# Fewer dummy products around the first transposes of a gated attention and SwiGLU kernel

## Chip, cores and metric

The kernel runs on one core of a Trainium2 chip. The metric is the device time of one execution in microseconds (us), lower is better. Before the change: 180.97 us, median of the three runs known when the prediction was written (180.55 to 181.46).

## The reference, cut to what matters

```python
def reference(A_x, A_wqkv, A_wo, B_x, B_w1, B_w3, B_w2, gate_w):
    x = A_x                                   # 1 x 2048 x 512, bf16
    g = sigmoid((x * gate_w).sum(-1, keepdims=True))
    a = linear_attention(x, A_wqkv, A_wo)     # q, k, v; phi(k)^T v and phi(q), 32 heads
    b = swiglu(x, B_w1, B_w3, B_w2)           # 512 -> 1376 -> 512
    return g * a + (1 - g) * b
```

Only the very first step counts here: keys of the first four token tiles, `k = x @ wk`, with x transposed on TensorE.

## The kernel before

Loads are issued on two queues. The first transposes need token tile 0 of x, the first key product needs the transposed tile and the first half of `wk`.

```python
dq = nc.sync
dq.dma_start(out=x_sb[:, 0:1, :], in_=x_r[:, 0:1, :])            # x tile 0
for i in range(2):                                               # wk, two halves
    kcs = slice(2 * i, 2 * i + 2)
    nc.scalar.dma_start(out=wk_sb[:, kcs, :], in_=wqkv_r[:, kcs, D : 2 * D])
dq.dma_start(out=x_sb[:, 1:2, :], in_=x_r[:, 1:2, :])            # x tile 1
dq.dma_start(out=x_sb[:, 2:TPB, :], in_=x_r[:, 2:TPB, :])        # x tiles 2 and 3
# ... later loads cut
warm_l = nc.const_aps.tensor(1.0, [P, P], BF16)
warm_r = nc.const_aps.tensor(1.0, [P, TB], BF16)                 # P = 128, TB = 512

def emit_warm(n):                                                # dummy products
    warm = psX.tile([P, TB], FP32, tag="XP3", name="warm")
    for i in range(n):
        nc.tensor.matmul(warm[:], lhsT=warm_l, rhs=warm_r, start=True, stop=True)

emit_warm(6)

def emit_xT(t):                  # 4 transposes of tile t, two copies back to SBUF
    for h in range(2):
        xTp = psX.tile([P, 2, P], BF16, tag=f"XP{(2 * t + h) % 3}", name="xTp")
        for j in range(2):
            kc = 2 * h + j
            nc.tensor.transpose(
                out=xTp[:, j, :], in_=x_sb[:, t, kc * P : (kc + 1) * P], identity=ident[:]
            )
        # ... h == 0: copy on VectorE, h == 1: copy on ScalarE
# ... cut
k0 = [psM.tile([P, D], FP32, tag="mm", name=f"k0_{t}") for t in range(TPB)]
emit_xT(0)
emit_warm(2)
emit_k_mm(k0[0], 0, 0)           # one product of 512 columns each
emit_k_mm(k0[0], 0, 1)
emit_xT(1)
emit_k_mm(k0[0], 0, 2)           # needs the second half of wk
emit_k_mm(k0[0], 0, 3)
emit_k_phi(k0[0], 0)
emit_xT(2)                       # needs x tiles 2 and 3, which land together
# ... then k tile 1, transposes of tile 3, k tiles 2 and 3, then the XP products (x^T @ phi(k))
```

TensorE (PE) starts its products in this order, so a step that waits holds up all those below it (in the trace before, the transposes of tile 0 wait until 3.41 us, and the two dummies below them, which need no load, start at 3.81).

## Time and profile before

Lines of the page of the kernel before. The second is the busy share of PE in 40 slices, in tenths; the third the granted clock; the last is the chain that ended last, by engine. PEld is TensorE's weight load, DVE is VectorE, ACT ScalarE, POOL GpSimd.

```profile
PE 175.5 (98%) x892; PEld 84.5 (47%) x892; DVE 118.9 (66%) x205; ACT 66.7 (37%) x126; POOL 61.2 (34%) x69
...
PE   8999999999999999999999999999999999999993
...
PEclk9999999999999999999999999999999999999999
...
PE 98%; DVE 0%; issue 0%; DVEq 0%
```

PE is the bound from end to end; only what moves its stream counts. One trap: the clock row says 9 in the first slice too, although the products there ran at half speed. The trace's clock record begins only at 5.88 us, and what lies before it is shown as if at full speed. The distance between starts tells the truth: 0.427 us for products before it, 0.216 after.

The timeline of the same kernel's start: start and duration in us, engine, line, operation, output and inputs, count, and in brackets the idle time before and what ended it.

```profile
0.84 2.72 PE L158 MATMUL warm<-const-bfloat16-1.0 128*128 128x512 bf16 x6 [0.84 <-PEq L471]
...
3.40 0.34 PEld L169 LDWEIGHTS <-x_sb 128*128 128x128 bf16 x4 [0.75 <-DMA x_sb<-in_A_x_dram]
3.41 0.61 PE L169 MATMUL xTp<-ident,x_sb 128*128 128x128 bf16 x4
...
3.81 1.06 PE L158 MATMUL warm<-const-bfloat16-1.0 128*128 128x512 bf16 x2
3.84 0.29 DVE L174 COPY xT<-xTp 128x256 bf16<-128x256 bf16 x1 [2.78 <-PE xTp L169]
...
4.66 1.06 PE L179 MATMUL k<-wk_sb,xT 128*128 128x512 bf16 x2
...
5.51 0.56 PE L169 MATMUL xTp<-ident,x_sb 128*128 128x128 bf16 x4
...
5.92 0.59 PE L179 MATMUL k<-wk_sb,xT 128*128 128x512 bf16 x2
...
6.35 0.39 PE L169 MATMUL xTp<-ident,x_sb 128*128 128x128 bf16 x4
```

Read the starts, since the durations include a modelled tail. Six dummies (0.84), four transposes (3.41), two dummies (3.81), the first two key products (4.66), transposes of tile 1 (5.51), two key products (5.92), transposes of tile 2 (6.35). Up to 5.8 us a product of 512 columns follows the last after 0.427 us and a transpose after 0.107; at full clock these are 0.216 and 0.056.

### The profile page before, as it was taken

What the parts mean: (1) busy time and instruction counts of PE and PEld (TensorE: products, weight loads), DVE (VectorE), ACT (ScalarE), POOL (GpSimd) and SP (SyncE); (2) the same over time, 40 slices, a digit from 0 to 9 for tenths busy, and PEclk for the clock granted to TensorE, in tenths of its full rate; (3) what the DMA queues carried; (4) which work ended last, traced back from release to release, by engine and by line L of the source; (5) the groups of instructions that cost most, each with busy time, mean ns of one, the idle gap of its engine ahead of it and who ended that gap; (6) DMA issues with size and microseconds to landing.
All of it is one profiled execution on the core that took longest, in us unless ns stands there. A gap on an engine that the chain in (4) does not pass through costs nothing.

```text
span 179.3 us, 2484 instructions
## 1 busy us (share of the span) xinstructions
PE 175.5 (98%) x892; PEld 84.5 (47%) x892; DVE 118.9 (66%) x205; ACT 66.7 (37%) x126; POOL 61.2 (34%) x69
## 2 busy tenths in 40 slices
PE   8999999999999999999999999999999999999993
PEld 3544444474444545444445444444545444444462
DVE  1598868596998837397787374978754669776000
ACT  4543322576624334343324343332443323331221
POOL 5177575645454323253003232620032328100000
PEclk9999999999999999999999999999999999999999
DMA  5999999901005010115000101240001013300011
GB/s 176 262 246 228 293 313 390 309 18 25 10 0 106 13 48 29 44 42 104 0 4 0 44 32 41 59 90 5 0 7 57 16 62 65 60 0 0 29 52 42
DMA packets 28285, 14.88 MB, mean 83 GB/s; under 512 B 19600, under 2 KB 27248, under 8 KB 28272
## 3 DMA queue, kind: packets, MB, share of 16 engines
q1 hardware_dynamic: 27728, 14.20, 29.5%
q10 hardware_dynamic: 544, 0.52, 0.8%
q8 instruction: 7, 0.11, 0.3%
q14 instruction: 6, 0.05, 0.1%
HBM read 8.42 MB, written 2.10 MB: 59 GB/s over the span
## 4 chain that ended last, share of the span: by engine, by line
PE 98%; DVE 0%; issue 0%; DVEq 0%
PE o_ps L350 19%; PE gate_ps L305 19%; PE up_ps L313 19%; PE XP L199 8%; PE o_ps L341 8%; PE q_ps L212 8%; PE k_ps L179 6%; PE r_ps L236 3%; PE k L179 2%; PE warm L158 2%; PE o_ps L345 2%; PE xTp L169 1%; PE kvT_ps L411 0%; PE W_ps L438 0%; DVE o_out L359 0%; PE z_ps L429 0%
## 5 line engine op out<-in xcount | busy, mean ns | idle before, releaser
L305 PE MATMUL gate_ps<-xT,w_sb 128*128 128x512 bf16 x160 | 41.1, 379 | 0.0
L313 PE MATMUL up_ps<-xT,w_sb 128*128 128x512 bf16 x160 | 41.1, 379 | 0.0
L220 POOL TENSOR_TENSOR qz<-pq,z_sb 128x512 f32<-128x512 bf16 x16 | 18.5, 1161 | 60.3 <-DVE pq L142 58.4
L318 ACT ACTIVATE th<-gate_ps 128x512 bf16<-128x512 f32 x40 | 23.9, 597 | 38.1 <-PE gate_ps L305 37.7
L350 PE MATMUL o_ps<-w_sb,hT 128*128 128x512 bf16 (+2 forms) x180 | 37.5, 355 | 0.0
L320 DVE SCALAR_TENSOR_TENSOR gs<-th,gate_ps 128x512 bf16<-128x512 bf16 x40 | 27.3, 683 | 5.8 <-ACT th L318 5.5
L323 DVE TENSOR_TENSOR hT<-up_ps,gs 128x512 bf16<-128x512 f32 x40 | 27.6, 691 | 3.8
L139 DVE TENSOR_SCALAR phi_m<-phi_e 128x512 bf16<-128x512 bf16 x32 | 14.9, 467 | 19.6 <-ACT phi_e L137 19.6
L350 PEld LDWEIGHTS <-hT 128*128 128x128 bf16 x180 | 16.8, 98 | 17.9
L313 PEld LDWEIGHTS <-w_sb 128*128 128x128 bf16 x160 | 15.7, 98 | 18.9
L305 PEld LDWEIGHTS <-w_sb 128*128 128x128 bf16 x160 | 15.6, 98 | 18.6
L355 ACT ACTIVATE o_out<-o_ps,omg 128x512 bf16<-128x512 f32 (+2 forms) x17 | 11.1, 656 | 30.4 <-PE o_ps L350 30.4
L285 POOL TENSOR_TENSOR pqn<-pq,rden 128x512 bf16<-128x512 bf16 x16 | 16.6, 1055 | 14.1 <-DVE rden L278 11.7
L189 POOL TENSOR_TENSOR pks<-pks,pk_sb 128x512 f32<-128x512 f32 x15 | 17.3, 1154 | 8.9 <-DVE pk_sb L142 8.4
L223 DVE TENSOR_REDUCE den<-qz 128x32 f32<-128x512 f32 x16 | 11.0, 685 | 8.9 <-POOL qz L220 8.9
L341 PE MATMUL o_ps<-W_sb,pqT 128*128 128x512 bf16 (+2 forms) x72 | 16.8, 355 | 0.0
L212 PE MATMUL q_ps<-wq_sb,xT 128*128 128x512 bf16 x64 | 16.3, 379 | 0.0
L199 PE MATMUL XP<-pk_sb,x_sb 128*128 128x512 bf16 x64 | 16.2, 379 | 0.0
L137 ACT ACTIVATE phi_e<-k_ps 128x512 bf16<-128x512 f32 x12 | 7.2, 597 | 15.4 <-PE k_ps L179 15.4
L179 PE MATMUL k_ps<-wk_sb,xT 128*128 128x512 bf16 x48 | 12.3, 379 | 0.0
L137 ACT ACTIVATE phi_e<-q_ps 128x512 bf16<-128x512 f32 x16 | 9.6, 597 | 7.0 <-PE q_ps L212 5.8
L142 DVE SCALAR_TENSOR_TENSOR pq<-q_ps,phi_m 128x512 bf16<-128x512 f32 x16 | 11.1, 691 | 0.5
(59 smaller groups left out, 120.7 us busy)
## 6 DMA issues: line engine op xcount, KB each, us to landing
w_sb<-in_B_w_dram SPq DMA_DIRECT2D x3, 1280.0 KB, 11.3
out_dram<-o_out SPq DMA_DIRECT2D x15, 128.0 KB, 1.7
x_sb<-in_A_x_dram SPq DMA_DIRECT2D x3, 512.0 KB, 4.6
wk_sb<-in_A_wqkv_dram ACTq DMA_DIRECT2D x2, 256.0 KB, 3.6
wq_sb<-in_A_wqkv_dram SPq DMA_DIRECT2D x1, 512.0 KB, 5.5
wv_sb<-in_A_wqkv_dram SPq DMA_DIRECT2D x1, 512.0 KB, 6.2
wo_sb<-in_A_wo_dram SPq DMA_DIRECT2D x1, 512.0 KB, 12.3
x_sb<-in_A_x_dram SPq DMA_DIRECT2D x2, 128.0 KB, 2.9
```

The lines of the kernel that those rows point to most:

```text
L179: nc.tensor.matmul(k_ps[:], lhsT=xT[:, kc, t * P : (t + 1) * P], rhs=wk_sb[:, kc, :], start=(kc == 0), stop=(kc == KC - 1),)
L189: nc.gpsimd.tensor_add(pks[:], pks[:], pk_sb[:, t, :])
L199: nc.tensor.matmul(XP_ps[dc][:], lhsT=x_sb[:, t, dc * P : (dc + 1) * P], rhs=pk_sb[:, t, :], start=(t == 0), stop=(t == NT - 1),)
L212: nc.tensor.matmul(q_ps[:], lhsT=xT[:, kc, ts_tok], rhs=wq_sb[:, kc, :], start=(kc == 0), stop=(kc == KC - 1),)
L220: nc.gpsimd.tensor_tensor(out=qz[:], in0=st[tb, "pq"][:, tt, :], in1=z_sb[:], op=ALU.mult)
L305: nc.tensor.matmul(gate_ps[:], lhsT=w1_sb[:, kc, fsl], rhs=xT[:, kc, tok_sl], start=(kc == 0), stop=(kc == KC - 1),)
L313: nc.tensor.matmul(up_ps[:], lhsT=w3_sb[:, kc, fsl], rhs=xT[:, kc, tok_sl], start=(kc == 0), stop=(kc == KC - 1),)
L318: nc.scalar.activation(out=th[:], in_=gate_ps[:], func=ACT.Tanh, scale=0.5)
L320: nc.vector.scalar_tensor_tensor(out=gs[:], in0=th[:], scalar=1.0, in1=gate_ps[:], op0=ALU.add, op1=ALU.mult)
L323: nc.vector.tensor_tensor(out=st[tb, "hT"][:, fc, :], in0=up_ps[:], in1=gs[:], op=ALU.mult)
L341: nc.tensor.matmul(o_ps[:], lhsT=st[tb, "pqT"][:, c, tsl], rhs=W_sb[:, c, a:b], start=(c == 0), stop=False,)
L350: nc.tensor.matmul(o_ps[:], lhsT=st[tb, "hT"][:, fc, tsl], rhs=w2_sb[:, fc, a:b], start=False, stop=(fc == FC - 1),)
```

## The change

The dummies keep PE active until the data are there. The intent is to have PE free sooner, ahead of the first transposes and ahead of the first key product.

```diff
-    def emit_warm(n):
+    def emit_warm(*widths):
         warm = psX.tile([P, TB], FP32, tag="XP3", name="warm")
-        for i in range(n):
-            nc.tensor.matmul(warm[:], lhsT=warm_l, rhs=warm_r, start=True, stop=True)
-
-    emit_warm(6)
+        for n in widths:
+            nc.tensor.matmul(
+                warm[:, 0:n], lhsT=warm_l, rhs=warm_r[:, 0:n], start=True, stop=True
+            )
+
+    emit_warm(TB, TB, TB, TB, TB, P, P)
 # ...
     emit_xT(0)
-    emit_warm(2)
+    emit_warm(TB)
     emit_k_mm(k0[0], 0, 0)
```

## The prediction

> **What bounds the kernel now.** The page's busy table has PE 98% busy (175.5 of 179.3 us); the chain that ended last is 98% PE and 0% issue. So only what moves PE's stream counts. The change touches the first 5 us.
>
> **The start as it is (timeline of the first 12 us and the chain there; single instructions read from the trace).** The first dummy starts at 0.84 us. Dummies start every 0.427 us, six of them, so the sixth has streamed by about 3.35. The four transposes of token tile 0 start at 3.41, one every 0.107; the waits view puts their weight load's wait on the DMA of x, whose last part landed at 3.36. Two dummies start at 3.81 and 4.24, the first key product at 4.66. Key products start every 0.427 until about 5.8, and every 0.216 from 5.92 on: the clock record says full clock from 5.88. [...]
>
> **What the change removes.** The order of PE instructions is otherwise the same.
> 1. Ahead of the transposes: 512 columns become 2 x 128, so 256 columns less, 0.427 - 2 x 0.107 = 0.213 us of cold stream; the dummies end near 3.14. But the transposes wait for x, landed at 3.36. I expect them at 3.40 still, and PE idle for about 0.27 us. Worth 0 where x lands as in this trace.
> 2. Between transposes and key product: one dummy less, 0.427 us. The key product needs the VectorE copy of the transposes, which ended at 4.13, and the first half of wk, landed at 4.08. After such a copy a weight load started 54 ns later elsewhere (8.394 to 8.448) and its product 72 ns after that. So I estimate the first key product at about 4.30 instead of 4.66: 0.36 us earlier, with 0.07 us of PE idle.
>
> **What reaches the end.** Later gates have slack: x tile 1 landed at 4.45 (needed at about 5.15), the second half of wk at 5.20 (needed at 5.58), x tiles 2 and 3 at 6.02 (needed near 6.17). If the clock still rises at about 5.88, 0.36 us of cold work more is done by then, which would have taken half of that at full clock: a gain of about 0.18 us, 0.1% of the time. PE does the rest unchanged.
>
> **The risk.** The dummies exist to keep PE active until the clock rises. In the window of 3.41 us that ended at 5.88, PE streamed about 98% of the time; after the change about 91%. [...] I think 91% passes, and give the bad case one chance in six. [...] those of before spread over 0.9 us, five times my gain.
>
> **Prediction: 180.8 us, 180.2 to 181.5 in 8 of 10.** Faster by over 2%: 0.01; within 2%: 0.98; slower: 0.01.
>
> **What would show it.** Right: transposes still at about 3.4 behind the DMA of x, with a new idle gap of 0.2 to 0.3 us; first key product near 4.3; products 0.427 apart until the clock record rises around 5 to 6.5 us; everything after that 0.2 us earlier. Wrong: transposes near 3.15 (x lands earlier than I read), or a rise of the clock beyond 7 us in the profile and slower times by 1 us or more.

The sum came to a gain of 0.18 us (0 from the first part; 0.36 us from the second, half of it kept), from 180.97 to 180.8 us. The price of the bad case (a later rise) was no part of the sum. An estimate of it from traces is 1.7 us, for products 0.427 instead of 0.216 us apart (measured before and after the rise) over 3.41 us, the difference between the clock records of before (174.08 us) and two_ahead (170.67 us, below). The "window of 3.41 us" is a stretch of that length. "Cold" stands for the 0.427 us.

## The result, and the profile after

The changed kernel took 180.76 us (median of six runs, 180.51 to 181.09) against 180.97 us (six runs, 180.55 to 181.46). The ratio is 0.9988 with a 95% interval of 0.9967 to 1.0009: the same time, within noise. Ratios here are the mean time of one kernel's runs over that of the other's of the same rounds, so not quite the ratio of the medians.

The timeline of the changed kernel's start, the lines that answer to those above:

```profile
0.84 2.51 PE L158 MATMUL warm<-const-bfloat16-1.0 128*128 128x512 bf16 x7 [0.84 <-PEq L473]
...
3.22 0.60 PE L171 MATMUL xTp<-ident,x_sb 128*128 128x128 bf16 x4
...
3.62 0.63 PE L158 MATMUL warm<-const-bfloat16-1.0 128*128 128x512 bf16 x1
3.65 0.29 DVE L176 COPY xT<-xTp 128x256 bf16<-128x256 bf16 x1 [2.59 <-PE xTp L171]
...
4.00 0.20 PEld L181 LDWEIGHTS <-xT 128*128 128x128 bf16 x2 [0.33 <-DVE xT L176]
4.05 1.00 PE L181 MATMUL k<-wk_sb,xT 128*128 128x512 bf16 x2
...
4.99 0.23 PEld L171 LDWEIGHTS <-x_sb 128*128 128x128 bf16 x4 [0.79 <-DMA x_sb<-in_A_x_dram]
4.99 0.40 PE L171 MATMUL xTp<-ident,x_sb 128*128 128x128 bf16 x4
...
5.46 0.59 PE L181 MATMUL k<-wk_sb,xT 128*128 128x512 bf16 x2
...
6.22 0.40 PE L171 MATMUL xTp<-ident,x_sb 128*128 128x128 bf16 x4 [0.17 <-DMA x_sb<-in_A_x_dram]
```

The first key product came 0.61 us earlier (4.05 against 4.66), but the transposes of tile 2 only 0.13 us earlier (6.22 against 6.35), and there PE waits for a load. The chain of waits in the first 12 us of the changed kernel (start, duration, what) says so:

```profile
1.72 4.46 DMA x_sb<-in_A_x_dram
6.17 0.05 issue
6.22 0.40 PE xTp L171 x4
6.62 0.86 PE k L181 x4
```

The chain now runs through the load of x tiles 2 and 3, which landed at 6.17 us, not through PE's stream from 0.84 us on. Two smaller waits lie before it in this trace. x tile 1 landed at 4.94 us (4.45 in the trace before) and held its transposes by 0.09 us, and the second half of `wk` landed at 5.42 us and held the key products at 5.46 by about 0.24 us. And the clock record rose at 4.86 us in this trace, a us earlier than before. Two questions follow: is the earlier clock an effect of the change, and how much of the 0.61 us does the load take back?

### The profile page after: what moved, and what is told of

It is laid out like the page before. It is cut to its first block, busy times and chain, and to the rows that moved or that the text cites. A ratio compares the mean times of both kernels' runs of the same rounds, so it can differ in the third digit from the quotient of the medians.

```text
span 179.1 us, 2484 instructions
## 1 busy us (share of the span) xinstructions
PE 175.0 (98%) x892; PEld 84.1 (47%) x892; DVE 117.8 (66%) x205; ACT 66.8 (37%) x126; POOL 61.5 (34%) x69
## 4 chain that ended last, share of the span: by engine, by line
PE 95%; DMA 2%; SPq 0%; DVE 0%; issue 0%; DVEq 0%
PE o_ps L352 19%; PE gate_ps L307 19%; PE up_ps L315 19%; PE o_ps L343 8%; PE XP L201 8%; PE q_ps L214 8%; PE k_ps L181 6%; PE r_ps L238 3%; DMA x_sb<-in_A_x_dram 2%; PE o_ps L347 2%; PE k L181 1%; PE kvT_ps L413 0%; PE W_ps L440 0%; PE xTp L171 0%; SPq L85 0%; SPq L81 0%
## 5 line engine op out<-in xcount | busy, mean ns | idle before, releaser
L139 DVE TENSOR_SCALAR phi_m<-phi_e 128x512 bf16<-128x512 bf16 x32 | 13.4, 419 | 20.7 <-ACT phi_e L137 20.5
```

## The experiments

**My theory.** The change gives PE time, but transposes of tile 2 start either when PE gets there or about 0.05 us after x tiles 2 and 3 land, whichever is later. The moment at which the clock rises sets which one it is. **Rivals.** The change does nothing at all; or the part ahead of the transposes gives the gain; or the change moved the clock's rise.

The readings of all traces stand here together. "Rise" is the start of the clock record, "x 2, 3" the last packet of that load (of tile 2 alone where the load is split), "tile 2" the start of its transposes, "XP" the start of the first XP product, all in us from the start of the span.

| run | rise | x tile 0 lands | first transpose | first k product | x 2, 3 land | tile 2 | XP | span |
|---|---|---|---|---|---|---|---|---|
| before | 5.88 | 3.36 | 3.41 | 4.66 | 6.02 | 6.35 | 9.38 | 179.34 |
| after | 4.86 | 3.17 | 3.22 | 4.05 | 6.17 | 6.22 | 9.27 | 179.09 |
| aa_before | 4.78 | 3.28 | 3.35 | 4.63 | 6.02 | 6.07 | 9.11 | 178.92 |
| after_again | 5.09 | 3.27 | 3.32 | 4.15 | 5.94 | 5.99 | 9.04 | 178.86 |
| second_only | 6.62 | 3.33 | 3.38 | 4.21 | 5.96 | 6.34 | 9.52 | 179.41 |
| first_only | 4.98 | 3.17 | 3.22 | 4.48 | 6.06 | 6.11 | 9.15 | 178.97 |
| no_dummies | 6.49 | 3.32 | 3.37 | 4.15 | 5.94 | 6.26 | 9.41 | 179.30 |
| two_ahead | 8.82 | 3.08 | 3.13 | 3.95 | 5.78 | 6.08 | 10.46 | 180.27 |
| six_between | no record | 2.94 | 3.35 | 5.24 | 5.79 | 6.32 | 9.36 | 179.30 |
| split_x | 6.04 | 2.97 | 3.14 | 3.99 | 5.35 | 6.09 | 9.12 | 179.00 |
| free_before | 4.00 | 2.86 | 3.35 | 4.33 | 6.01 (not used) | 5.41 | 8.45 | 178.40 |
| free_after | 3.49 | 2.90 | 3.14 | 3.94 | 6.07 (not used) | 5.04 | 8.08 | 178.02 |
| split_x_before | 5.52 | 2.98 | 3.35 | 4.63 | 5.27 | 6.16 | 9.20 | 179.10 |
| split_x_again | 6.02 | 3.02 | 3.14 | 3.99 | 5.66 | 6.08 | 9.12 | 179.00 |

From the first XP product to the end all of these take 169.81 to 169.96 us. So whatever the change does, it does before that product, and that column can be compared where the times are too noisy.

### The kernel against itself, and the change again

No edit for aa_before; the changed kernel for after_again.

> The unchanged kernel, timed against itself, for the size of the noise and a second trace of its start. If the start differs between executions of one kernel (clock rise, landing of x) then its clock record will rise at another time than 5.88 us, and the ratio will still be 1.000 within 0.2%. If the starts of one kernel are alike, the rise is at 5.9 us again and x tile 0 lands at 3.36 us again; then the earlier rise (4.86 us) and the earlier landing (3.18 us) in the changed kernel's trace would be effects of the change.

> The whole change again. My theory (PE gains what the dummies took, until it meets the landing of x tiles 2 and 3 at about 6.1 us): 0.1 to 0.25 us faster than before, ratio 0.9986 to 0.9995; transposes of tile 2 at 6.2 us whatever the clock does. Rival (the change does nothing, the first difference was noise): ratio 1.000, as near to 1 as the kernel against itself.

Measured: aa_before 180.76 us median, ratio 1.0010 (0.9993 to 1.0027). after_again 180.85 us, ratio 1.0011 (0.9996 to 1.0026). The change stands where the kernel against itself stands; my expected ratio of 0.9986 to 0.9995 was not met, and my "6.2 us whatever the clock does" should have been "0.05 us after the load lands" (5.99 here). The chain of aa_before, then that of after_again:

```profile
1.72 4.30 DMA x_sb<-in_A_x_dram
6.02 0.05 issue
6.07 0.40 PE xTp L169 x4
...
1.72 4.22 DMA x_sb<-in_A_x_dram
5.94 0.05 issue
5.99 0.40 PE xTp L171 x4
```

In this execution the unchanged kernel had the earlier clock (4.78) and waited for the same load. So the earlier clock is not an effect of the change. In the four traces with an early rise and these loads in the way (after, aa_before, after_again, and first_only below), tile 2 starts 0.05 us after the landing, whichever kernel it is. The fairest pair is aa_before and after_again, with rises of 4.78 and 5.09: the first key product comes 0.48 us earlier with the change (4.15 against 4.63), tile 2 only 0.08 us earlier, and that is the difference between the two landings.

### One part of the change at a time

```diff
 second_only:  -emit_warm(TB, TB, TB, TB, TB, P, P)   +emit_warm(TB, TB, TB, TB, TB, TB)
 first_only:   -emit_warm(TB)  # after emit_xT(0)     +emit_warm(TB, TB)
```

> Only the dummy between transposes and first key product is taken away; six full ones stand ahead. My theory: this is the part that counts; first key product about 0.84 us after the first transpose (1.25 before), a gain of 0.1 to 0.2 us, ratio about 0.999, as the whole change. Rival (the part ahead of the transposes gives the gain): ratio 1.000.

> Only the dummies ahead are shortened by 256 columns; two stand between. My theory: first transpose earlier by 0 to 0.2 us, by as much as x tile 0 lands ahead of 3.35 us; ratio between 0.9992 and 1.000. Rival (the part ahead gives the gain): ratio about 0.9985.

Measured: second_only 180.74 us, ratio 0.9998 (0.9985 to 1.0011). first_only 181.00 us, ratio 1.0018 (1.0003 to 1.0032). The times settle nothing; the interval of first_only lies just above 1, but the kernel against itself gave 1.0010 beside it, and its trace, which fell on the fastest of its six runs, shows no lost time. I leave it as unexplained and small. The traces do separate the parts. From the first transpose to the first key product: 1.26 us with two dummies (before, aa_before, first_only: 1.25 to 1.28), 0.83 us with one (after, after_again, second_only). That 0.43 us is a whole dummy of 512 columns. The part ahead moves the first transpose from 3.35 at the earliest to whatever x tile 0 allows: 3.22 in first_only, 3.22 and 3.32 in the changed kernel, and 3.14 in the three traces below in which x tile 0 landed by 3.02 (free_after, split_x, split_x_again): 0.03 to 0.21 us.

The clock rose late in second_only (6.62), and the chain there has no load in it:

```profile
5.70 0.85 PE k L181 x2
6.55 0.32 PE xTp L171 x4
6.87 0.86 PE k L181 x4
```

(The chain counts a piece from the modelled end of the one before, so it shows 6.55 where the start is 6.34.) x tiles 2 and 3 had landed at 5.96; PE came later. That is the other branch of the theory.

### Taking dummies away

```diff
 no_dummies:  -emit_warm(TB, TB, TB, TB, TB, P, P)   and   -emit_warm(TB)
 two_ahead:   -emit_warm(TB, TB, TB, TB, TB, P, P)   +emit_warm(TB, TB)
```

> No dummy products at all. My theory (dummies are worth their place only through the clock; the first transpose waits for x and the first key product for the VectorE copy anyway): first transpose at 3.2 to 3.4 us and first key product about 0.83 us later, as in the changed kernel, but the clock rises between 6.5 and 10 us, tile 2's transposes start at 6.2 to 6.7 us, and the time is 0.5 to 1.8 us longer, ratio 1.003 to 1.010. Rival (dummies do nothing): ratio 1.000 and the clock rise at about 5 us.

> Two full dummies ahead, then PE idle from 1.7 us to the landing of x at about 3.25 us, one dummy between. [...] (the window that ended at 3.2 us in the trace of second_only would have been 69% busy and did not raise the clock; those that did were 95% or more): the clock rises between 6.2 and 10 us and the time is as without dummies, ratio 1.003 to 1.010. Rival (any activity since 0.84 us counts): rise between 4.7 and 6.7 us, ratio 1.000.

Measured: no_dummies 181.55 us, ratio 1.0050 (1.0012 to 1.0088). two_ahead 181.67 us, ratio 1.0041 (1.0012 to 1.0070). Both times are as expected: the dummies are worth about 0.8 us. That they work through the clock is seen in the trace of two_ahead (rise 8.82, XP at 10.46). The trace of no_dummies fell on the fastest of its four runs (181.01 us) and shows no loss (rise 6.49, XP at 9.41 against 9.38 before), so for its slower runs a late rise is argued, not seen. The chain of two_ahead shows the half-speed stretch at its price:

```profile
5.44 0.85 PE k L181 x2
6.29 0.43 PE xTp L171 x4
6.72 1.71 PE k L181 x4
8.42 0.43 PE xTp L171 x4
8.85 1.77 PE k L181 x8
```

Four key products took 1.71 us before the rise at 8.82, eight took 1.77 mostly after it. And no_dummies shows what the first key product waits for when nothing stands between it and the transposes:

```profile
3.37 0.41 PE xTp L170 x2
3.78 0.02 issue
3.80 0.30 DVE xT L175
4.10 0.05 issue
4.15 1.03 PE k L180 x2
```

0.78 us after the first transpose, against 0.83 with one dummy: the VectorE copy holds it, so the one remaining dummy costs 0.05 us at most.

**What stood before the rise.** Every complete clock record is 174.08 us long, but for two_ahead's, which is 170.67. The two differ by 3.41 us, and are 51 and 50 times 3.4133. I took this length for a stretch that ended at the rise, which is an assumption, and worked out the share of it in which PE streamed columns (each product from its start, for 0.427 us per 512 columns before the rise), and the same for the stretch before it:

| run | 3.41 us that ended at the rise | 3.41 us before that (no rise at its end) |
|---|---|---|
| before | 0.98 | 0.48 |
| after | 0.98 | 0.18 |
| after_again | 0.95 | 0.25 |
| second_only | 0.99 | 0.69 |
| two_ahead | 1.00 | 0.67 |
| no_dummies | 0.80 | 0.00 |
| free_after (below) | 0.78 | 0.00 |

The six other traces with a record agree (0.93 to 1.00, and at most 0.52 before). So in these thirteen traces the clock rose after stretches with shares of 0.78 to 1.00, and did not after stretches with 0.00 to 0.69; by what rule it rises they do not show. Transposes made up about 0.31 of the 0.80 in no_dummies and 0.10 of the 0.78 in free_after (estimates by the same reckoning). With the changed kernel the share before the rise was 0.95 or more in after and after_again, and the rise came at 4.86 and 5.09 us, so the idle gap that the change opens (0.08 and 0.18 us ahead of the transposes) is harmless in these traces. I did not test a longer gap.

### Adding dummies

```diff
-    emit_warm(2)
+    emit_warm(6)
```
in the kernel before, after `emit_xT(0)`.

> Four full dummies more between transposes and first key product than before. My theory (the dummies sit in a slack of a few tenths of a us ahead of the landing of x tiles 2 and 3, and cost their full time beyond it): 4 x 0.43 us less what runs at full clock (0.22 each) less a slack of 0.3 us: tile 2's transposes at 7.0 to 7.7 us, time longer by 0.8 to 1.5 us, ratio 1.004 to 1.009. Rival (dummies between are off the critical path altogether): ratio 1.000.

Measured: 181.49 us, ratio 1.0037 (1.0004 to 1.0069); the means differ by 0.68 us. The rival (off the critical path) falls, if narrowly by the interval. The trace, of the fastest of its four runs, shows the cost in one place: in spite of an early clock PE came to tile 2 at 6.32, after the landing at 5.79. My 7.0 to 7.7 us for tile 2 missed: in this trace the products go from 0.427 to 0.22 us apart near 4.1 us, so the added dummies ran mostly at full clock, and tile 2 started at 6.32. The clock's draw again.

### Splitting the load of x tiles 2 and 3

```diff
-    dq.dma_start(out=x_sb[:, 2:TPB, :], in_=x_r[:, 2:TPB, :])
+    for t in range(2, TPB):
+        dq.dma_start(out=x_sb[:, t : t + 1, :], in_=x_r[:, t : t + 1, :])
```
in the changed kernel (split_x, split_x_again) and in the kernel before (split_x_before).

> The changed kernel with the load of x tiles 2 and 3 split in two, so that tile 2 lands ahead of tile 3. My theory (where the clock rises early, tile 2's transposes wait for the pair's landing): tile 2 lands at 5.5 to 5.7 us, its transposes start right after the last products of k tile 0 (about 5.8 us if the clock rises near 5), and the time is 0.1 to 0.3 us shorter than before: ratio 0.998 to 0.9995. Rival (the landing is not what holds the start): ratio as the changed kernel's, 1.000 within 0.001, with transposes of tile 2 no earlier than 6.0 us.

> The kernel before, with the load of x tiles 2 and 3 split. My theory: tile 2 lands at about 5.4 us instead of 6.0 with tile 3, so tile 2's transposes start when PE gets there (5.8 us for a rise at 4.8, 6.35 for 5.9). Mean 0.15 to 0.2 us below before, ratio 0.999.

> The changed kernel with the load split, again. My theory: the change and the split together gain 0.25 to 0.35 us on the mean, ratio 0.998 to 0.9987, and 0.15 us ahead of split_x_before. Rival (the split gives nothing, x's landing is not the wait): as the changed kernel, ratio 0.9995 to 1.000. A mean difference of 0.15 us is about what five rounds can just tell.

Measured: split_x 180.78 us, ratio 0.9991 (0.9966 to 1.0015). split_x_before 181.00 us, ratio 1.0004 (0.9981 to 1.0026), where I had expected 0.999. split_x_again 180.26 us, ratio 0.9972 (0.9949 to 0.9995). Tile 2 lands at 5.27 to 5.66 us instead of about 6.0. In all three traces the clock rose at 5.5 us or later, and PE, not the load, came last, so no trace shows the split at work where it was meant to help. The chain of split_x_again:

```profile
5.05 0.43 PE xTp L172 x4
5.47 0.77 PE k L182 x2
6.24 0.22 PE xTp L172 x4
```

These traces show what the change is worth where the clock rises late. split_x and split_x_again rose at 6.04 and 6.02 us, before at 5.88; in all three PE's arrival came last (tile 3 too had landed, at 6.01 and 5.86). Yet XP starts at 9.12 against 9.38: 0.26 us earlier in spite of a later clock. The split itself had no part in that, but x tile 0 had: it landed at 2.97 and 3.02 us, against 3.36. For a rise at 6.0 the arithmetic of "The sum" puts the change at 0.32 us with x tile 0 at 2.97 and at 0.22 us with 3.36 (estimates).

With the load split in both kernels the change does show in the times. The twelve runs of split_x and split_x_again have a mean of 180.55 us, the six of split_x_before 180.96, on the same chip: 0.40 us, with a 95% interval of about 0.14 to 0.67. That is more than the 0.15 us that I had expected, and split_x_before came out above before (180.86) where I had put it below, so some of it is the luck of the draw.

### Without the loads in the way

Wrong on purpose (relative error 0.021): every transpose reads x tile 0, and k tile 0 takes the first half of wk only.

```diff
-  in_=x_sb[:, t, kc * P : (kc + 1) * P]
+  in_=x_sb[:, 0, kc * P : (kc + 1) * P]
-  rhs=wk_sb[:, kc, :]
+  rhs=wk_sb[:, kc if t else kc % 2, :]
```

> The kernel before, wrong on purpose: all transposes read x tile 0, and k tile 0 uses the first half of wk only, so nothing up to the first XP product waits for x tiles 1 to 3 or the second half of wk. My theory: PE's own stream alone sets the start; with the clock rise at R (3.5 to 6.8 us) the first XP product starts at about 8.84 us for R = 4.8, 9.13 for 5.4, 9.42 for 6.0 (worked out from the products' durations at both clocks). Mean time 0.1 to 0.4 us below before, ratio 0.998 to 0.9995.

> The same two waits taken out of the changed kernel (wrong on purpose). My theory (the landings absorb most of what the change gains): without them the change is worth 0.21 us on the mean instead of 0.09; first XP product at about 8.60 us for a rise at 4.8, 8.89 for 5.4, 9.19 for 6.0, each 0.24 us ahead of free_before at the same rise, and ahead of 9.03 us, below which no trace with the waits came. Rival (the change gains nothing even without the waits): the same start as free_before at the same rise; ratio of the two 1.000.

Measured: free_before 180.50 us median, ratio 0.9989 (0.9960 to 1.0017). free_after 180.21 us, ratio 0.9962 (0.9935 to 0.9990). The means are 180.60 and 180.21 against 180.86 of before. With its loads out of the way the changed kernel is measurably faster than before, where with them it was not; but freeing the loads gave the kernel before 0.26 us too, by the means (the interval of free_before includes 1). The 0.39 us between the two has runs spread by over 1 us in each, so it fits the expected 0.21 but doesn't prove it. Both start XP (8.45 and 8.08) ahead of 9.04, the earliest of any trace with the waits. The chain of free_after has no load at all; tile 2's transposes start at 5.04, which no trace with the waits comes near:

```profile
3.94 0.60 PE k L181 x2
4.55 0.22 PE xTp L171 x4
4.77 0.43 PE k L181 x2
5.20 0.22 PE xTp L171 x4
```

### The sum

With the four measured steps (0.427 and 0.107 us, 0.216 and 0.056 at full clock), the landing times of each trace plus 0.05 us, the VectorE copy, and the rise of each trace, I recomputed the start of the first XP product. It comes out within 0.03 us in all thirteen traces with a clock record, so nothing else of size is at work there. The same arithmetic with landings of 3.27, 4.38 and 6.02 us, averaged over rises that I assume to be spread evenly between 3.45 and 6.85 us (the eleven traces with five or more dummies ahead and a record rose between 3.49 and 6.62), is an estimate of the mean effect:

| clock rise | before, XP at | changed, XP at | gain |
|---|---|---|---|
| 4.8 us or earlier | 9.10 | 9.10 | 0.00 |
| 5.4 us | 9.13 | 9.10 | 0.03 |
| 6.0 us | 9.42 | 9.19 | 0.23 |
| 6.6 us | 9.72 | 9.48 | 0.24 |
| mean of all rises | 9.27 | 9.18 | 0.09 |

The second part gives 0.08 us of it alone, the first 0.01. Without the waits for x tiles 1 to 3 and the second half of wk the mean gain would be 0.21 us, and change and split together would give 0.35 us. Measured for the last: twelve runs of split_x and split_x_again have a mean of 180.55 us, 0.30 us under the 180.86 of before on the same chip. That is the best version found, by 0.2%; one of its two intervals reaches over 1, so I call it likely and not shown.

## Why the prediction was right

The time, 180.76 us, lies in the range, beside the predicted 180.8, and within 2%. That is a weak test: the range also held 180.97, no change at all, and the noise is larger than the effect. Right as well: PE's stream as the bound outside the start, the half-speed start, the small size, and that the clock would still rise with the added idle time (at 4.86 us). But of the signs that the prediction named, most did not come: the transposes started at 3.22 and not 3.4, the idle gap was 0.08 us and not 0.2 to 0.3, the first key product came at 4.05 and not 4.3, and XP came 0.12 us earlier and not 0.2. That the number came so close is luck: more was gained ahead of the first key product than predicted, and loads took most of it back. Several steps were off, and they matter for the next such question.

1. *"I expect them at 3.40 still, and PE idle for about 0.27 us. Worth 0."* The transposes started at 3.22, as x tile 0 landed at 3.17 in that trace. Over the traces it landed between 2.86 and 3.36 us. One trace's landing is a draw, not a constant; the part is worth 0.03 to 0.21 us ahead of the transposes.
2. *"First key product at about 4.30 instead of 4.66: 0.36 us earlier, with 0.07 us of PE idle."* It came 0.83 us after the first transpose, where my two figures made it 0.90; the full 0.43 us was gained, with no idle. In this trace the weight load started at 4.00 and the product at 4.05, before that load's 0.10 us were over; I had counted on more.
3. *"Later gates have slack ... x tiles 2 and 3 at 6.02 (needed near 6.17)."* This step failed. In both traces of the changed kernel PE reached that point at about 5.7 to 5.9 us and waited until 5.99 and 6.22. In the first of them (after) x tile 1 (4.94) and the second half of `wk` (5.42) held PE too. My 0.15 us of slack held only for the one clock rise that I had seen.
4. *"If the clock still rises at about 5.88 ... a gain of about 0.18 us."* It did not: 4.86 and 5.09. The rise moves between executions of one kernel too (5.88 and 4.78 in the two traces of the kernel before). Where it is late the change is worth 0.2 to 0.3 us, where it is early nothing, and the mean is about half of what I predicted (estimate 0.09 us). Neither is told from zero by the times: 12 runs of the changed kernel have a mean of 180.84 us, and the runs of before, on several chips, 180.84 us too.
5. *"I think 91% passes, and give the bad case one chance in six."* With the change the clock rose after 3.41 us with PE streaming for 95% and 98%, and in free_after after 78%; neither trace of the changed kernel shows a rise beyond 5.09 us, and its slowest of twelve runs (181.37 us) is no slower than the slowest of before (181.48).

## What to carry to other kernels

At a kernel's start find the gate behind the one that you relax: where the clock rose early, a key product moved forward by 0.48 us, and the next tiles, whose load had almost no slack, started with their load as before. Before reading a difference between two traces of a start, take a second trace of the same kernel: landings moved by half a us and, in the kernel before, the clock's rise by 1.1 us, more than the change itself. And dummies before the data arrive cost 0.03 to 0.21 us at most here and are worth about 0.8 us, while those between the data and the real work cost their stream time wherever PE, and not a load, comes last at the next gate (four more of them cost 0.68 us, by the means).
